# Attention rounds of a fused retention-and-MLP kernel: one state per round, whole rounds, and a ninth unit transposed by TensorE

## The chip, the core and the metric

The kernel runs on one core of a Trainium2 chip. A core has TensorE (PE in the profile; its weight loads are PEld), VectorE (DVE), ScalarE (ACT), GpSimd (POOL) and SyncE (SP), with 16 DMA engines. The time is the device time of one execution in microseconds (us). A comparison uses the median of several runs.

## What is computed

The reference is a retention layer without softmax, followed by an MLP with exact GELU. The shapes are q, k, v of (8, 8, 576, 64) (batch, heads, positions, head size), w_in (512, 2048), w_out (2048, 512) and an output of (4608, 512).

```python
scores = scale * np.matmul(q, k.transpose(0, 1, 3, 2))
gamma = 1.0 - 2.0 ** (-5.0 - np.arange(H))
rel = pos[:, None] - pos[None, :]
Dmat = np.where(rel >= 0, gamma[:, None, None] ** rel[None], 0.0)
attn_out = np.matmul(scores * Dmat[None], v)
x = attn_out.transpose(0, 2, 1, 3).reshape(B * S, H * D)
h = x @ w_in
out = (0.5 * h * (1.0 + erf(h / np.sqrt(2)))) @ w_out
```

## The kernel before

**Units and groups.** The 576 positions are cut into chunks of 128: four whole ones (ci = 0 to 3) and a tail of 64 (ci = 4). Batches go in pairs (bp = 0 to 3; j is the member of the pair). A unit is one chunk of one batch with all eight heads; the two tails of a pair share a unit. There are 36 units, numbered in the order of work, each 128 token columns of xT. Units 0, 1 are the chunk ci = 0 of bp = 0, and 2, 3 that of bp = 1. Then come 4 to 10 (rest of bp = 0), 11 to 17 (rest of bp = 1), 18 to 26 (bp = 2), 27 to 35 (bp = 3). Units with ci = 0 are called raw: they have no earlier chunk to add. Units 2 and 3 are also called kept, because their inputs stay loaded until bp = 1 begins. A group is the two units of one (bp, ci), or the tail alone.

**Steps of a unit.** Each has a function of its own:
- `load`: three DMAs issued by GpSimd bring q, k, v, cast to bf16.
- `turn` (TensorE into PSUM, line 294, then a copy by ScalarE or VectorE) or `turn_dma` (one DMA transpose issued by SP, line 303) makes qkT. The first N_PE_TR units take `turn`.
- `scores`: eight TensorE products (line 317) into two PSUM banks.
- `masked`: two VectorE products with the mask (line 332) give ret.
- `scaled_v`: VectorE scales v by a decay (line 342) and gives vh; the planner's time for it is called V. A raw unit's `inner` takes v itself, but the state needs its vh.
- `inner`: eight TensorE products of ret with the values (line 354) into a bank o_ps.
- `state`, once per group of two: 16 TensorE products (line 372) add k and vh to the running state in the bank u_ps, which is kept from ci = 0 to ci = 3. Two copies by ScalarE or VectorE (lines 284, 282) then bring it to u_sb.
- `cross`: four products with the state of the chunk before, or eight of half the width for a tail unit (line 406), added to o_ps.
- `evacuate`: o_ps goes to xT (line 426; for raw units by `either`, lines 282 and 284).

**The MLP.** The 4608 tokens form nine blocks of 512 columns, four units each. `mlp1` makes hT from w_in and xT (line 445), and ScalarE applies GELU (line 451). `mlp2` makes four output tiles per block from g and w_out (line 484), which ScalarE copies to o_sb (line 489) and SP sends out (line 492).

**The order.** Nothing is scheduled at run time. A planner in the kernel's Python code keeps a clock for each engine (T) and due times for loads, transposes, masks, copies and PSUM banks, and writes out the one order in which all engines get their instructions. At each step of its main loop it issues the first candidate that is due, else the next MLP piece whose inputs are due. The candidates before the change are X (cross and evacuate), U (a state), B (inner products, then all states that are due), A (scores of a group, with the inner products, states and crosses of the units before it) and T (a TensorE transpose). nT, nA, nB and nX count the units transposed, scored, with inner products and with crosses; units nB to nA - 1 are therefore scored and waiting for their inner products. A round is such a set issued together between two MLP pieces. "Early" means fewer than four units scored. "Stuck" means that the next MLP piece is due over 0.5 us from now. From block 2 on, A is offered only before the second or third piece of an `mlp2` output tile.

Two details matter below. Before the change, A issues every state whose V is planned at all:

```python
while u_due and state_at(*u_due[0]) < 1e8:
    state(*u_due[0])
```

And a stuck A takes one unit of the group:

```python
if early or stuck:
    g = g[:1]
```

There are eight PSUM banks, nine buffers for loaded units, eight for qkT and four for output tiles. Each state or tail unit that is done calls for the loads of later units (`reload`).

Of the kernel before, what the change touches and what calls it, by code (L numbers as in the profile page):

```python
# [17 lines left out]
def kernel(  # L18
# [16 lines left out]
    B, H, S, D = q.shape  # L35
# [9 lines left out]
    N_BLK = n_tok // TOK  # L45
# [13 lines left out]
    N_U = len(units)  # L59
# [5 lines left out]
    n = v_order.index(pair_of[1, 1][0])  # L65
    v_order[n:n] = kept

    N_PE_TR = 8
    N_LD = 9
    N_QKT = 8  # L70
    N_VH = 6
# [176 lines left out]
    def frees(n):  # L248
        got = sorted((x for x in banks if x not in held), key=lambda x: free_at[x])
        return got[:n]  # L250

    def free_time(n):
        got = frees(n)
        return free_at[got[-1]] if len(got) == n else 1e9
# [45 lines left out]
    def turn_dma(i):  # L300
        s = st[i]
        s["qkT"] = tr_pool.tile([128, 2, HP, 128], BF16, tag="qkT", name="qkT")
        nc.sync.dma_start(s["qkT"].rearrange("p j hp s -> p (j hp) s"),
                          loaded[i][0].rearrange("p j h d -> p (j h d)"), transpose=True)
        at = on("sp", 1.3, max(land["q", i], land["k", i]))
        turned[0] = max(turned[0], at) + 3.1
        sw[0] = max(sw[0], at) + 2.2
        s["T", 0] = s["T", 1] = turned[0] + 3.4

# [36 lines left out]
    def inner(i):  # L346
        bp, ci, j = units[i]
        s = st[i]
        s["o"] = bank([128, HP, 128], FP32, "o_ps")
        o = s["o"][1]  # L350
        vals = loaded[i][1] if i in raw else s["vh"]
        for hp in range(HP):
            for e in range(2):
                nc.tensor.matmul(o[64 * e:64 * e + 64, hp, :], lhsT=vals[:, 2 * hp + e, :], rhs=s["ret"][e][:, hp, :],  # L354
                                 start=(hp == 0), stop=(ci == 0 and hp == HP - 1), skip_group_check=True)
        s["B"] = pe(0.23, "col")
        s["Bdone"] = True
        if j is None:
            s_done.add(i)
        elif j == 1 and ci < NCI - 1 and (bp, ci) != (1, 0):  # L360
            u_due.append((bp, ci))
# [25 lines left out]
                reload()  # L387

    def state_at(bp, ci):
        return max(st[i].get("V", 1e9) if "Bdone" in st[i] else 1e9 for i in pair_of[bp, ci])  # L390

    def reload():
        ORDER.extend(f"{what}{next_load[0]}" for what in "qkv")
# [146 lines left out]
    def fire():  # L540
        nonlocal nT, nV
        now = T["pe"]
        while ORDER and T["pool"] <= now + 1.5:
            next_order()
        for key in [x for x in cast_due if land[x] <= now + 0.2]:
            dst, src = cast_due.pop(key)
            land[key] = either(0.44, land[key], dst, src) + SEM
        while later:
            n = next((n for n, x in enumerate(later) if x[0] <= now and T[x[1]] <= now + 0.05
                      and (x[1] == "dve" or later[0][3] is not make_args)), None)  # L550
            if n is None:
                break
            _, engine, dur, fn = later.pop(n)
            fn()
            on(engine, dur, now)
        while nV < N_U and nV < len(s_done) + N_VH and ("v", v_order[nV]) in land:
            i = v_order[nV]
            if land["v", i] + 0.1 > now or nA <= i or i in kept and nA < 8 or i in raw and T["dve"] > now:
                break
            scaled_v(i)  # L560
            nV += 1
        while (N_PE_TR <= nT < N_U and nT < nX + N_QKT - 1 and ("k", nT) in land
               and land["k", nT] + 0.3 <= now):
            turn_dma(nT)
            nT += 1
# [14 lines left out]
    while True:  # L580
        fire()
        now = T["pe"]
        acts = []

        def cand(ready, fn, *a):
            acts.append((ready, fn, a))

        pick = mlp_pick(1 if runs and runs[0] and runs[0][0][1] > 1 else 4)
        head = pick[1][0] if pick else None
        early = nA < 4  # L590
        stuck = bool(pick) and pick[0] > now + 0.5

        if nX < nB:
            bp, ci, j = units[nX]
            cand(u_ready.get((bp, ci - 1), 1e9) if ci else 0.0, "X")
        for key in u_due[:1]:
            if nA < 8 or nA == N_U or nB == nA:
                cand(state_at(*key), "U", *key)
        if nB < nA:
            g = [nB] if early else list(range(nB, nA))  # L600
            ready = max(max(st[i]["R"], land["v", i] if i in raw else st[i].get("V", 1e9)) for i in g)
            ready = max(ready, free_time(len(g) + (units[nB][1] == 0 and units[nB][2] == 0)))
            hurry = early or nA == N_U or stuck
            if not hurry and runs and runs[0]:
                kind, t = runs[0][0][0], runs[0][0][1]
                hurry = nB < 4 * t + 4 if kind == "1" else len(runs[0]) <= 6 and nB < 4 * t + 8
            if hurry:
                cand(ready, "B", g)
        if nA < N_U:
            g = [i for i in groups[group_of[nA]] if i >= nA]  # L610
            if early or stuck:
                g = g[:1]
            if all(("T", 1) in st[i] and ("T", 0) in st[i] for i in g):
                ready = max(max(st[i]["T", 0], st[i]["T", 1]) for i in g)
                back = [i for i in range(nB, nA) if st[i]["R"] <= now and (i in raw or "V" in st[i])]
                n = 2 * len(g) + len(back)
                ok = nA - nB <= 2
                if early or stuck:
                    cand(max(ready, free_time(2)) if ok else 1e9, "A", g, [])
                elif head is None or head[1] == 0 or head[0] == "2" and 4 <= head[3] <= 8 and head[1] < N_BLK - 1:  # L620
                    if len(back) == nA - nB and (head is None or nA + len(g) <= 4 * head[1] + AHEAD + 2 * (head[1] > 1)):
                        cand(max(ready, free_time(min(n, 8 - len(held))) - 0.3), "A", g, back)
        if nT < N_PE_TR and nT <= nA + 3:
            key = ("qk"[half], nT)
            if key in land and key not in cast_due:
                cand(max(land[key] + 0.05, free_time(1)), "T", nT, half)
        due = [a for a in acts if a[0] <= now]
        if due:
            _, kind, a = due[0]
            if kind == "X":  # L630
                cross(nX)
                evacuate(nX)
                nX += 1
            elif kind == "U":
                state(*a)
            elif kind == "B":
                for i in a[0]:
                    inner(i)
                    nB += 1
                while u_due and state_at(*u_due[0]) <= T["pe"]:  # L640
                    state(*u_due[0])
            elif kind == "A":
                g, back = a
                for i in back:
                    inner(i)
                    nB += 1
                while u_due and state_at(*u_due[0]) < 1e8:
                    state(*u_due[0])
                for i in g:
                    scores(i)  # L650
                    nA += 1
                for n, i in enumerate(g):
                    masked(i)
                    if n == 0:
                        for x in back:
                            cross(x)
                            evacuate(x)
                            nX += 1
            elif kind == "T":
                turn(*a)  # L660
                half = 1 - half
                nT += 1 - half
            continue
        if pick and pick[0] <= now:
            one = pick[1].pop(0)
            (mlp1 if one[0] == "1" else mlp2)(*one[1:])
            continue
        waits = [a[0] for a in acts] + ([pick[0]] if pick else [])
        soon = [x for x in (land[key] for key in cast_due)]
        if nV < N_U and ("v", v_order[nV]) in land and nV < len(s_done) + N_VH:  # L670
            soon.append(land["v", v_order[nV]] + 0.1)
        if N_PE_TR <= nT < N_U and ("k", nT) in land and nT < nX + N_QKT - 1:
            soon.append(land["k", nT] + 0.3)
        waits = [w for w in waits + soon if w > now and w < 1e8]
        if not waits:
            break
        gap = min(waits) - now
        if now < 16 and gap > 0.2:
            warm(max(1, round(gap / (0.43 if now < HOT else 0.23))))
        T["pe"] = max(T["pe"], min(waits))  # L680
# [31 lines left out]
```

## Time and profile before

| | before |
|---|---|
| median of 3 runs | 307.11 us (306.79 to 308.41) |
| the profiled execution | 307.32 us |
| its span, first to last instruction | 305.6 us |
| granted TensorE clock | 1.000 |
| TensorE busy | 296.2 us, 97% |
| ScalarE busy | 135.7 us, 44% |
| GpSimd busy | 113.8 us, 37% |
| VectorE busy | 99.7 us, 33% |
| largest groups: hT products, oT products | 127.9 and 123.5 us |

Busy time is the time in which at least one instruction of the engine was in flight. Matmuls overlap in the pipeline, so a product's own duration (0.38 us for 512 columns) is longer than the step from one to the next. What a block of work costs TensorE is therefore read from starts: the start of the next block less its own. In a line of waits, the two names are the waiting instruction and what ended the wait, and the numbers are the total, the count and the longest. Times in the timeline run from the span's start.

### The profile page before, as it was taken

The page shows a single profiled execution, that of the slowest core. Times are in us where ns is not written, and L with a number is a line of the kernel's source. Part 1 is how long each engine was busy: PE and PEld are TensorE (multiplying, and loading weights), DVE is VectorE, ACT ScalarE, POOL GpSimd, SP SyncE. Part 2 cuts the span into 40 slices and gives each one's busy share as a digit, 9 for nine tenths or more (in the row PEclk, how much of TensorE's full clock was granted, in tenths as well). Part 3 has the DMA queues.
Part 4 walks back from the last instruction along what each step waited for, and adds up shares of the span by engine and source line. Part 5 has one row for each costly group of instructions (what it writes and reads, how often), then busy time and mean ns, then how long its engine had stood idle before and what let it go on. Part 6 is the DMA issues. An engine that isn't in the chain of part 4 may idle for free. (4 is left out here: it accounts for less than half of the span.)

```text
span 305.6 us, 5759 instructions
## 1 busy us (share of the span) xinstructions
PE 296.2 (97%) x2391; PEld 160.3 (52%) x2425; DVE 99.7 (33%) x187; ACT 135.7 (44%) x243; POOL 113.8 (37%) x143
## 2 busy tenths in 40 slices
PE   7999999999999999999998999999989999999996
PEld 2589675765544554454444554444444544544445
DVE  6864325036530560055004670180008600400000
ACT  5575444433367234631562236422661266217611
POOL 8987895865349654200307944300000000000000
PEclk9999999999999999999999999999999999999999
DMA  9999999999999999995918999992000210010022
GB/s 140 164 182 188 176 183 151 216 169 175 172 176 145 154 186 158 176 116 115 126 21 55 159 150 174 172 157 94 9 2 34 66 39 2 34 71 34 0 65 75
DMA packets 154042, 35.77 MB, mean 117 GB/s; under 512 B 143008, under 2 KB 149536, under 8 KB 154016
## 3 DMA queue, kind: packets, MB, share of 16 engines
q0 software_dynamic: 116832, 18.10, 86.8%
q1 hardware_dynamic: 36144, 17.05, 28.9%
q8 instruction: 19, 0.31, 0.4%
q10 hardware_dynamic: 1040, 0.26, 0.4%
q14 instruction: 7, 0.06, 0.1%
HBM read 36.70 MB, written 9.44 MB: 151 GB/s over the span
## 5 line engine op out<-in xcount | busy, mean ns | idle before, releaser
L445 PE MATMUL hT<-xT,w_in 128*128 128x512 bf16 (+2 forms) x758 | 127.9, 325 | 0.8 <-DVE xT L426 0.2
L484 PE MATMUL oT<-w_out,g 128*128 128x512 bf16 x538 | 123.5, 379 | 1.2 <-issue 0.2
L451 ACT ACTIVATE g<-hT 128x512 bf16<-128x512 f32 (+1 forms) x152 | 86.9, 574 | 48.1 <-PE hT L445 47.6
L445 PEld LDWEIGHTS <-w_in 128*128 128x128 bf16 x768 | 69.6, 98 | 56.8 <-DVE xT L426 0.4
L484 PEld LDWEIGHTS <-g 128*128 128x128 bf16 x560 | 53.4, 98 | 60.2
L489 ACT COPY o_sb<-oT 128x512 f32<-128x512 f32 x35 | 20.4, 586 | 92.8 <-PE oT L484 74.8
L332 DVE TENSOR_TENSOR ret<-sc,msk 128x512 bf16<-128x512 f32 x56 | 35.5, 684 | 63.0 <-PE sc L317 63.0
L219 POOL DMA_DIRECT2D qk_ld<-in_q_dram x31 | 27.9, 901 | 42.2 <-DMA qkT<-qk_ld 15.8
L219 POOL DMA_DIRECT2D v_ld<-in_v_dram x32 | 28.8, 900 | 13.0 <-DMA qk_ld<-in_q_dram 8.4
L219 POOL DMA_DIRECT2D qk_ld<-in_k_dram x31 | 28.0, 903 | 5.6 <-DMA v_ld<-in_v_dram 3.7
L342 DVE TENSOR_TENSOR vh<-v_ld,dv 128x512 bf16<-128x512 bf16 x36 | 23.4, 684 | 1.9 <-DMA v_ld<-in_v_dram 1.9
L284 ACT CAST u_sb<-u_ps 64x512 bf16<-64x512 f32 x26 | 15.1, 579 | 15.5 <-PE u_ps L372 15.2
L332 DVE TENSOR_TENSOR ret<-sc,near 128x512 bf16<-128x512 f32 x16 | 10.3, 685 | 35.4 <-PE sc L317 35.4
L426 DVE TENSOR_TENSOR xT<-o_ps,dqT 128x512 bf16<-128x512 f32 x28 | 18.2, 683 | 10.8 <-PE o_ps L406 10.8
L282 DVE CAST u_sb<-u_ps 64x512 bf16<-64x512 f32 x6 | 4.1, 688 | 45.7 <-PE u_ps L372 45.6
L317 PE MATMUL sc<-qkT 64*128 64x128 bf16 x288 | 12.3, 220 | 0.0
L354 PEld LDWEIGHTS <-vh 128*64 128x64 bf16 x224 | 6.8, 109 | 7.4 <-issue 5.9
L317 PEld LDWEIGHTS <-qkT 64*128 64x128 bf16 x288 | 8.2, 95 | 3.2 <-issue 1.1
L354 PE MATMUL o_ps<-ret,vh 128*64 128x128 bf16 x224 | 9.7, 223 | 0.0
L372 PE MATMUL u_ps<-vh,qk_ld 128*64 128x64 bf16 x256 | 6.8, 196 | 2.8 <-ACT u_sb L284 2.5
L406 PE MATMUL o_ps<-qkT,u_sb 128*128 128x128 bf16 (+1 forms) x128 | 9.3, 214 | 0.0
L215 POOL DMA_DIRECT2D v_ld<-in_v_dram x8 | 5.4, 678 | 10.0 <-DMA v_ld<-in_v_dram 3.9
(51 smaller groups left out, 99.8 us busy)
## 6 DMA issues: line engine op xcount, KB each, us to landing
out_dram<-o_sb SPq DMA_DIRECT2D x31, 256.0 KB, 4.1
v_ld<-in_v_dram POOLq DMA_DIRECT2D x32, 128.0 KB, 8.8
qk_ld<-in_k_dram POOLq DMA_DIRECT2D x31, 128.0 KB, 9.1
qk_ld<-in_q_dram POOLq DMA_DIRECT2D x31, 128.0 KB, 8.7
w_in<-in_moe_w_in_dram POOLq DMA_DIRECT2D x8, 256.0 KB, 7.5
w_out<-in_moe_w_out_dram POOLq DMA_DIRECT2D x8, 256.0 KB, 8.2
out_dram<-o_sb SPq DMA_DIRECT2D x9, 128.0 KB, 2.4
qk_ld<-in_q_dram POOLq DMA_DIRECT2D x8, 64.0 KB, 11.6
```

The lines of the kernel that those rows point to most:

```text
L219: nc.gpsimd.dma_start(dst, src[2 * bp + j, :, ci * C:ci * C + C, :].rearrange("h s d -> s h d"))
L284: nc.scalar.copy(dst, src)
L317: nc.tensor.matmul(got[e][1][:, hp, :], lhsT=qkT[sl, 1, hp, :], rhs=qkT[sl, 0, hp, :], start=True, stop=True)
L332: nc.vector.tensor_tensor(r, t, by, op=ALU.mult)
L342: nc.vector.tensor_tensor(vh, loaded[i][1], dv[:, :, ci:ci + 1].to_broadcast([128, H, D]), op=ALU.mult)
L354: nc.tensor.matmul(o[64 * e:64 * e + 64, hp, :], lhsT=vals[:, 2 * hp + e, :], rhs=s["ret"][e][:, hp, :], start=(hp == 0), stop=(ci == 0 an ...
L406: nc.tensor.matmul(o[:, hp, cols], lhsT=u[:, jj, hp, :], rhs=s["qkT"][:, 0, hp, cols], start=False, stop=(hp == HP - 1), skip_group_check= ...
L426: nc.vector.tensor_tensor(dst, o, by, op=ALU.mult)
L445: nc.tensor.matmul(hT[:, m, :], lhsT=w[:, cc, o:o + 128], rhs=xT[:, cc, t * TOK + lo:t * TOK + hi], start=(cc == 0), stop=(cc == N_DM - 1))
L451: nc.scalar.activation(g_tiles[t, m0 // 2][:, m0 % 2:m0 % 2 + n, lo:hi], hT, AF.Gelu)
L484: nc.tensor.matmul(oT, lhsT=g_tiles[t, m // 2][:, m % 2, cols], rhs=w_out_sb[m // 2][:, m % 2, :], start=(m == 0), stop=(m == N_DF - 1))
L489: nc.scalar.copy(o_sb, oT)
```

## The change

1. N_PE_TR goes from 8 to 9: unit 8 is transposed by TensorE, no longer by a DMA.
2. The planner's due time for a DMA transpose is later when many loads are queued in front of it.
3. A state counts as due only when the state before it has been copied to u_sb (`state_at`), and a round issues at most one state.
4. `scaled_v` of a raw unit may be put on VectorE when that engine is planned up to 2 us behind (once nA > 8); before, VectorE had to be idle.
5. Candidates A and B become one, S. It issues the inner products of all waiting units, one state, the scores of the next group, the mask of the group's first unit, the crosses of the waiting units and the other mask. When stuck, the masks all come after the crosses.
6. A round wants R (mask) and V due for all waiting units, raw ones too. A stuck step after the start takes the whole group. Rounds are also offered in the second cut of block 1's `mlp1`.

```diff
-    N_PE_TR = 8
+    N_PE_TR = 9
...
-        turned[0] = max(turned[0], at) + 3.1
+        busy = sw[0] > at + 1.0
+        turned[0] = max(max(turned[0], at) + 3.1, turned[0] + 4.4 * busy, at + 5.4 * busy)
...
     def state_at(bp, ci):
-        return max(st[i].get("V", 1e9) if "Bdone" in st[i] else 1e9 for i in pair_of[bp, ci])
+        at = u_ready.get((bp, ci - 1), 1e9) if ci else 0.0
+        return max([at] + [st[i].get("V", 1e9) if "Bdone" in st[i] else 1e9 for i in pair_of[bp, ci]])
...
-            if land["v", i] + 0.1 > now or nA <= i or i in kept and nA < 8 or i in raw and T["dve"] > now:
+            if land["v", i] + 0.1 > now or nA <= i or i in kept and nA < 8 or i in raw and T["dve"] > now + 2.0 * (nA > 8):
...
+        g, scored = [], 1e9
+        if nA < N_U:
+            g = [i for i in groups[group_of[nA]] if i >= nA]
+            if early or stuck and nA < 8:
+                g = g[:1]
+            if all(("T", 1) in st[i] and ("T", 0) in st[i] for i in g):
+                scored = max(max(st[i]["T", 0], st[i]["T", 1]) for i in g)
+        back = list(range(nB, nA))
         if nB < nA:
...
+            ready = max(max(st[i]["R"], land["v", i] if i in raw and nA < 8 else st[i].get("V", 1e9)) for i in back)
+            ready = max(ready, free_time(len(back) + first_o))
...
             if hurry:
-                cand(ready, "B", g)
...
+                n = len(back) + first_o + 2 * len(g)
+                along = not early and nA >= 4 and scored <= now and len(frees(n)) == n and free_time(n) <= now + 0.3
+                cand(ready, "S", g if along else [], back)
+        if g and scored < 1e8:
             if early or stuck:
...
+                cand(max(scored, free_time(2 * len(g))) if nA - nB <= 2 else 1e9, "S", g, [])
+            elif head is None or head[1] == 0 or head[1] == 1 and head[0] == "1" and head[4] > 0 or head[0] == "2" and 4 <= head[3] <= 8 and head[1] < N_BLK - 1:
+                if (all(st[i]["R"] <= now and st[i].get("V", 1e9) <= now + 0.3 for i in back)
+                        and (head is None or nA + len(g) <= 4 * head[1] + AHEAD + 2 * (head[1] > 1))):
+                    n = 2 * len(g) + len(back)
+                    cand(max(scored, free_time(min(n, 8 - len(held))) - 0.3), "S", g, back)
...
+            elif kind == "S":
                 g, back = a
                 for i in back:
                     inner(i)
                     nB += 1
-                while u_due and state_at(*u_due[0]) < 1e8:
+                if back and u_due and state_at(*u_due[0]) <= T["pe"] + 0.3 * (nA >= 8):
                     state(*u_due[0])
                 for i in g:
                     scores(i)
                     nA += 1
...
+                if not stuck:
+                    for i in g[:1]:
+                        masked(i)
+                if not early and nX == nB - len(back):
+                    for x in back:
+                        cross(x)
+                        evacuate(x)
+                        nX += 1
+                for i in g[not stuck:]:
+                    masked(i)
```

More of the change, by code (lines that the diff above doesn't have):

```diff
@@ L598 @@
                 cand(state_at(*key), "U", *key)
-        if nB < nA:
-            g = [nB] if early else list(range(nB, nA))
-            ready = max(max(st[i]["R"], land["v", i] if i in raw else st[i].get("V", 1e9)) for i in g)
-            ready = max(ready, free_time(len(g) + (units[nB][1] == 0 and units[nB][2] == 0)))
+        g, scored = [], 1e9
[6 more added lines that the diff above has]
+        back = list(range(nB, nA))
+        if nB < nA:
+            if early:
+                back = [nB]
+            first_o = units[nB][1] == 0 and units[nB][2] == 0
+            ready = max(max(st[i]["R"], land["v", i] if i in raw and nA < 8 else st[i].get("V", 1e9)) for i in back)
+            ready = max(ready, free_time(len(back) + first_o))
             hurry = early or nA == N_U or stuck
@@ L607 @@
             if hurry:
-                cand(ready, "B", g)
-        if nA < N_U:
-            g = [i for i in groups[group_of[nA]] if i >= nA]
+                n = len(back) + first_o + 2 * len(g)
+                along = not early and nA >= 4 and scored <= now and len(frees(n)) == n and free_time(n) <= now + 0.3
+                cand(ready, "S", g if along else [], back)
+        if g and scored < 1e8:
             if early or stuck:
[L612 to L622, printed above, removed]
+                cand(max(scored, free_time(2 * len(g))) if nA - nB <= 2 else 1e9, "S", g, [])
[4 more added lines that the diff above has]
+                    cand(max(scored, free_time(min(n, 8 - len(held))) - 0.3), "S", g, back)
         if nT < N_PE_TR and nT <= nA + 3:
@@ L635 @@
                 state(*a)
[L636 to L642, printed above, removed]
+            elif kind == "S":
                 g, back = a
@@ L651 @@
                     nA += 1
-                for n, i in enumerate(g):
-                    masked(i)
[L654 to L658, printed above, removed]
+                if not stuck:
[7 more added lines that the diff above has]
+                for i in g[not stuck:]:
+                    masked(i)
             elif kind == "T":
```

## Prediction, made before the change was run

> **What bounds the kernel now.** I read the page first.
>
> ```profile
> PE 296.2 (97%) x2391; PEld 160.3 (52%) x2425; DVE 99.7 (33%) x187; ACT 135.7 (44%) x243; POOL 113.8 (37%) x143
> ...
> PEclk9999999999999999999999999999999999999999
> ```
>
> TensorE is occupied for 97% of the span at full granted clock, every other engine under half. So the time is the sum of what TensorE issues, plus the places where it stands still; anything on another engine counts only if TensorE ends up waiting for it. Next, TensorE's waits, which say where it stands still.
>
> ```profile
> PE u_ps L372 <- ACT u_sb L284: 2.5, 2, 1.3
> PE warm L577 <- DVE zeros L100: 1.2, 1, 1.2
> PE u_ps L372 <- PE o_ps L354: 0.3, 1, 0.3
> PE hT L445 <- DVE xT L426: 0.2, 1, 0.2
> ```
>
> After the start there is one wait of size, twice: a state update (u_ps) waiting for ScalarE's copy of the state before. No line is a wait for a load or a transposed input: DMA, 90% busy or more in most slices of the first two thirds, is hidden. Third, TensorE's timeline gives the attention blocks between MLP products. A block's cost is the start of the next MLP product less the start of its own first product (columns: start, duration, engine, line, operation).
>
> ```profile
> 40.52 0.61 PE L294 MATMUL qk_ps<-ident,qk_ld 128*128 128x128 bf16 x8
> 40.96 1.04 PE L445 MATMUL hT<-xT,w_in 128*128 128x256 bf16 x8
> ...
> 136.08 0.64 PE L354 MATMUL o_ps<-ret,v_ld 128*64 128x128 bf16 x16
> 136.65 0.62 PE L317 MATMUL sc<-qkT 64*128 64x128 bf16 x16
> 137.20 9.67 PE L484 MATMUL oT<-w_out,g 128*128 128x512 bf16 x43
> ...
> 161.48 0.64 PE L354 MATMUL o_ps<-ret,vh 128*64 128x128 bf16 x16
> 161.95 0.42 PE L372 MATMUL u_ps<-vh,qk_ld 128*64 128x64 bf16 x16
> 163.64 0.44 PE L372 MATMUL u_ps<-vh,qk_ld 128*64 128x64 bf16 x16 [1.27 <-ACT u_sb L284]
> 164.02 0.62 PE L317 MATMUL sc<-qkT 64*128 64x128 bf16 x16
> 164.57 0.62 PE L406 MATMUL o_ps<-qkT,u_sb 128*128 128x128 bf16 x8
> 165.24 6.86 PE L484 MATMUL oT<-w_out,g 128*128 128x512 bf16 x31
> ...
> 172.03 0.64 PE L354 MATMUL o_ps<-ret,vh 128*64 128x128 bf16 x16
> 172.50 0.42 PE L372 MATMUL u_ps<-vh,qk_ld 128*64 128x64 bf16 x16
> 172.85 0.62 PE L317 MATMUL sc<-qkT 64*128 64x128 bf16 x16
> 173.40 0.62 PE L406 MATMUL o_ps<-qkT,u_sb 128*128 128x128 bf16 x8
> 174.07 1.24 PE L484 MATMUL oT<-w_out,g 128*128 128x512 bf16 x5
> ```
>
> A normal whole round (two inner products, one state, two scores, two crosses) takes 174.07 - 172.03 = 2.04 us. The round at 161.48 takes 3.76: two states stand in it, and the second writes the bank that ScalarE still copies. The round of the ci = 0 pair before it (136.08) takes 1.12 and has no state. The same pair of rounds comes back at 201.06 (1.12) and 226.46 (3.76).
>
> **The state rounds: -2.9 us.** The ci = 0 pairs at issue are 18, 19 (bp = 2) and 27, 28 (bp = 3). Three edits act together. scaled_v of such a pair no longer waits for VectorE to be idle, a round waits for V of its pair, and a round issues one state, if the state before it is already copied. So state (2,0) moves from the round at 161.48 into the one at 136.08, and by the next round its two copies (0.58 us each) have been done for long. A state within a round costs 0.25 (172.50 to the scores, 0.35, less the 0.11 that changing tile mode costs: eight scores take 0.33, sixteen 0.55, so 0.22 a unit and 0.11 fixed). Before: 1.12 + 3.76 = 4.88; after: 1.37 + 2.04 = 3.41. That saves 1.47 each, 2.9 for both. What is late next: the moved state reads vh of its pair. If VectorE is behind, the state waits, and the scores, crosses and all MLP products queued behind it wait too. The planner allows 0.3 us of lateness; the nearest rows are four weight-load waits on vh, 1.5 us in all, none over 0.4. I bound it by 0 and 0.4 per round and take 0.1 each, **+0.2**.
>
> What else moves with the state: its reloads. GpSimd waited 15.1 us at 147 to 162 for that state before it issued the next loads; they now go about 25 us earlier, into slices in which DMA was not full (tenths 5, 9 and 1 from 138 to 160). Nothing waits for these loads, so this is slack and no time; SP's transposes of them come earlier among the output DMAs, which four o_sb buffers, one used per 3.45 us of products, cover. If that cover went, an output copy would wait behind one transpose issue (1.2 to 4.2 us on SP). The state bank is held some 25 us longer, through an MLP stretch of 64 products: such a stretch took 13.82 us with a state bank held (84.59 to 98.41) and 13.81 without (116.62 to 130.43), so zero.
>
> **Whole rounds between 65 and 135 us: -0.8 us.** Blocks before, from the timeline: 0.55 (8, 9 scored), 1.82, 1.72 (10, then 11, 12), 2.00 (11, 12, then 13 alone, with 0.23 idle for xT), 0.91 (13; 14), 1.38 (14; 15, 16), 2.03 (15, 16; 17, slow by 0.21 against its twin of 1.82), 1.36. Sum 11.77. After, following the planner's branches by hand: 8, 9 are scored in the second cut of block 1's MLP1 (0.55), then 1.82, then 10 with 11, 12 as one round (1.38, as at 103.83), then 11, 12 (1.28, as at 51.26), 13, 14 scored together (0.55), one whole round (2.04), 1.82, 1.36. Sum 10.80, so -0.97. Between 11, 12 and MLP1 of block 2 lies the copy to xT: if no MLP2 piece is left to hide it, about 0.6 more are idle, unless 13 and 14 are scored in it. Bounds -0.4 and -1.0; I take -0.8, near the end that the rows add up to.
>
> **Scores of 8 and 9 some 4 us earlier: 0.** Their transposes must have landed. Unit 9's landed at 60.6 and its scores stood at 65.7; the new slot is near 61.8. One transpose fewer lies ahead of it in DMA. Transposes took 3.0 to 11.3 us to land, 8.2 this one, so the bounds are 0 and 1.5 us of standing still, with all MLP1 behind it; I take 0, since the slot stays behind the row's landing time.
>
> **Ninth unit by TensorE: +0.45 us.** Eight transposes took 40.96 - 40.52 = 0.44, without a change of mode; two copies (0.42 on VectorE or 0.59 on ScalarE) fall where VectorE is 29% and ScalarE 45% busy (40 to 60 us) and 4 us before the scores are due. They take two of eight PSUM banks for a microsecond: bounds 0.44 and 0.9 should an MLP1 product wait for a bank. Removed: one DMA transpose (issue 1.33 on SP, 41.74 to landing 50.15). The loads queued behind it should come about 2 us earlier. TensorE waits for none of them: nothing gained.
>
> [...]
>
> The constants turned and busy only delay the planner's idea of a transpose; units from 14 on were scored over 9 us after landing, so zero.
>
> **Sum.** -2.9 + 0.2 - 0.8 + 0 + 0.45 = -3.05. The profiled execution took 307.32 us (span 305.6 and 1.7 around it): 304.3. The median of the runs is 0.2 lower; I predict 304.0 for a median. About 0.5%, 1.5 us, is what a measurement of this kernel can tell from no change.
>
> **Rivals.**
> *Late transposes.* The earlier scores of 8, 9, or 13, 14 wait in TensorE's queue for the DMA: 1 to 2 us. For: transposes landed up to 11.3 us after issue, and unit 14's landed at 84.4, beside where 13, 14 could now be scored. Against: one transpose less ahead. 305 to 306. Chance 0.11.
> *The state does not move.* VectorE, with masks, xT and vh of one round queued (139.48 is where vh ran before), stays too late for the ci = 0 round, and the two waits only change their place: 307.3 - 0.8 + 0.45 = 307.0, median 306.8. Chance 0.08.
> *State lag, slower.* One state per round also means that a missed one stays a round behind. Then each cross waits for the two copies just started: 1.18 + 0.2 less 0.55 of scores, about 0.85 a round, in up to four rounds of each of two sequences: 6.8, in place of 2.9. It decides from four such rounds on; with all eight, 307.3 + 6.8 - 2.9 - 0.8 + 0.45 = 310.9. For: the while loop that caught up is gone. Against: rounds lie 5 us and more apart, and copies take 1.2. Chance 0.07.
> Main case: 0.74, 303.2 to 305.0.
>
> **How the numbers follow.** Low end: no vh wait (-0.2), all of -0.97, and a little of idle issue, 303.0. High end: through the late transposes, 306.2; left out are the last two rivals (0.15) and some 0.05 below. Under 305.6 lie the main case and about half of the late transposes: faster 0.80. Same: the other half and most of the second rival, 0.12. Slower 0.08.
>
> **What would show it.** Right: the u_ps wait on u_sb gone; 16 state products between inner products and scores in both ci = 0 rounds, block near 1.37; the next round near 2.04; no eight-score block of unit 13; 72 transposes on line 294's counterpart instead of 64. Wrong: a wait of sc on a DMA transpose, of o_ps on u_sb in every round, or of u_ps on vh over 0.4; or MLP blocks that lengthen.

## The result

| | before | changed |
|---|---|---|
| median | 307.17 us (306.79 to 308.41) | 303.75 us (303.28 to 304.56) |
| runs | 4 | 4 |
| profiled execution | 307.32 us | 303.70 us |
| its span | 305.6 us | 301.9 us |

The ratio of the times is 0.9885, with a 95% interval of 0.9849 to 0.992. The prediction was 304.0 us, between 303.0 and 306.2. On another chip the changed kernel came out at 304.22 us beside 307.37 for the one before, a ratio of 0.9894 (0.988 to 0.9909).

The first two lines are from the page of the changed kernel.

```profile
PE 295.3 (98%) x2400; PEld 160.6 (53%) x2433; DVE 99.1 (33%) x188; ACT 136.6 (45%) x244; POOL 114.1 (38%) x143
...
PEclk9999999999999999999999999999999999999999
```

TensorE is still the bound (98% busy) and still at full granted clock (1.000). It was busy 0.9 us less in a span 3.7 us shorter. Most of the gain is therefore standing still that is gone, as TensorE's waits say (total, count, longest):

```profile
PE warm L579 <- DVE zeros L100: 1.2, 1, 1.2
PE oT L486 <- issue: 0.3, 2, 0.2
PE u_ps L373 <- PE o_ps L355: 0.3, 1, 0.3
```

The two waits of u_ps for the copy to u_sb, 2.5 us together, have no successor in this list. TensorE's timeline shows the rounds (start, duration, engine, line, operation):

```profile
40.30 0.61 PE L294 MATMUL qk_ps<-ident,qk_ld 128*128 128x128 bf16 x8
...
42.48 0.39 PE L294 MATMUL qk_ps<-ident,qk_ld 128*128 128x128 bf16 x4
42.70 1.04 PE L447 MATMUL hT<-xT,w_in 128*128 128x256 bf16 x8
43.58 0.39 PE L294 MATMUL qk_ps<-ident,qk_ld 128*128 128x128 bf16 x4
43.80 1.04 PE L447 MATMUL hT<-xT,w_in 128*128 128x256 bf16 x8
...
98.76 0.62 PE L318 MATMUL sc<-qkT 64*128 64x128 bf16 x16
99.31 4.49 PE L486 MATMUL oT<-w_out,g 128*128 128x512 bf16 x19
...
130.66 0.41 PE L355 MATMUL o_ps<-ret,vh 128*64 128x128 bf16 x8
...
136.22 0.64 PE L355 MATMUL o_ps<-ret,v_ld 128*64 128x128 bf16 x16
136.69 0.42 PE L373 MATMUL u_ps<-vh,qk_ld 128*64 128x64 bf16 x16
137.04 0.62 PE L318 MATMUL sc<-qkT 64*128 64x128 bf16 x16
137.81 8.58 PE L486 MATMUL oT<-w_out,g 128*128 128x512 bf16 x39 [0.16 <-issue]
...
161.00 0.64 PE L355 MATMUL o_ps<-ret,vh 128*64 128x128 bf16 x16
161.47 0.42 PE L373 MATMUL u_ps<-vh,qk_ld 128*64 128x64 bf16 x16
161.82 0.62 PE L318 MATMUL sc<-qkT 64*128 64x128 bf16 x16
162.38 0.62 PE L408 MATMUL o_ps<-qkT,u_sb 128*128 128x128 bf16 x8
163.05 6.85 PE L486 MATMUL oT<-w_out,g 128*128 128x512 bf16 x31
...
226.56 6.85 PE L486 MATMUL oT<-w_out,g 128*128 128x512 bf16 x31
```

Unit 8's transposes are the two groups of four at 42.48 and 43.58, each 0.22 us from its start to the next product's. Units 13 and 14 are scored together at 98.76. The round of the ci = 0 pair at 136.22 now holds a state, and the round at 161.00 holds one instead of two: 163.05 - 161.00 = 2.05 us, where 3.76 stood.

One thing has to be known for reading blocks. The trace lacks some matmul records: the page of the changed kernel has 560 weight loads of line 486 but 537 products, and a later profile of the same kernel has 560 of both. Where the first MLP product after a block is missing, the block reads one product, 0.21 us, too long. That is so at 137.81 (39 records of 40 products) and at 163.05 (31 of 32), and at 165.24 and 174.07 in the trace of before (31 of 32 and 19 of 20). In the profile of the run with the state rule alone, where the record is there, a whole round is 1.84 us (161.78 to 163.62), not 2.04. Differences between blocks that miss the same record hold.

The shortening of 3.7 us, cut at points that are the same in both traces (the points of the kernel before that were not shown yet):

```profile
131.39 0.41 PE L354 MATMUL o_ps<-ret,vh 128*64 128x128 bf16 x8
...
230.22 6.86 PE L484 MATMUL oT<-w_out,g 128*128 128x512 bf16 x31
```

| stretch | before | changed | difference |
|---|---|---|---|
| start to the transposes of unit 7 | 40.52 | 40.30 | -0.22 |
| from there to the round of unit 17 (131.39, 130.66) | 90.87 | 90.36 | -0.51 |
| to the MLP product after the round of 20, 21 (165.24, 163.05) | 33.85 | 32.39 | -1.46 |
| to the one after the round of 29, 30 (230.22, 226.56) | 64.98 | 63.51 | -1.47 |
| to the end | 75.38 | 75.34 | -0.04 |

The -0.51 contains the 0.44 of the ninth unit; without it, whole rounds gave -0.95. The -0.22 belongs to no edit. TensorE's instructions up to there come in the same order. The first MLP product began at 14.48 before and at 14.26 in the changed kernel, and between 13.9 and 15.1 us in the profiles of the other runs.

### The profile page after: what moved, and what is told of

Same layout as the page of the kernel before. It is cut to its first block, busy times and chain, and to the rows that moved or that the text cites. A ratio compares the mean times of both kernels' runs of the same rounds, so it can differ in the third digit from the quotient of the medians.

```text
span 301.9 us, 5775 instructions
## 1 busy us (share of the span) xinstructions
PE 295.3 (98%) x2400; PEld 160.6 (53%) x2433; DVE 99.1 (33%) x188; ACT 136.6 (45%) x244; POOL 114.1 (38%) x143
## 4 chain that ended last, share of the span: by engine, by line
PE 98%; issue 1%; DVE 0%; ACT 0%
PE hT L447 41%; PE oT L486 40%; PE o_ps L355 4%; PE sc L318 3%; PE o_ps L408 3%; PE qk_ps L294 2%; PE warm L579 2%; PE warm L572 1%; PE u_ps L373 1%; PE oT L473 1%; DVE zeros L100 0%; ACT o_sb L477 0%
## 5 line engine op out<-in xcount | busy, mean ns | idle before, releaser
L219 POOL DMA_DIRECT2D v_ld<-in_v_dram x32 | 28.6, 893 | 14.1 <-DMA qk_ld<-in_q_dram 4.1
L219 POOL DMA_DIRECT2D qk_ld<-in_k_dram x31 | 27.9, 902 | 7.8 <-DMA v_ld<-in_v_dram 6.0
L284 ACT CAST u_sb<-u_ps 64x512 bf16<-64x512 f32 x29 | 16.8, 580 | 21.1 <-PE u_ps L373 19.8
L282 DVE COPY qkT<-qk_ps 128x512 bf16<-128x512 bf16 x14 | 5.8, 422 | 8.5 <-PE qk_ps L294 8.4
L215 POOL DMA_DIRECT2D qk_ld<-in_k_dram x8 | 5.5, 693 | 6.7 <-DMA qk_ld<-in_k_dram 3.7
L408 PEld LDWEIGHTS <-u_sb 128*128 128x128 bf16 x128 | 6.5, 98 | 1.5
```

The source lines that it names most:

```text
L219: nc.gpsimd.dma_start(dst, src[2 * bp + j, :, ci * C:ci * C + C, :].rearrange("h s d -> s h d"))
L284: nc.scalar.copy(dst, src)
L408: nc.tensor.matmul(o[:, hp, cols], lhsT=u[:, jj, hp, :], rhs=s["qkT"][:, 0, hp, cols], start=False, stop=(hp == HP - 1), skip_group_check= ...
```

## The experiments

### The state rule, alone and undone

The kernel before got the slack for VectorE and the wait for V, the latter limited to the pairs of bp = 2 and 3:

```diff
-  ... or i in raw and T["dve"] > now:
+  ... or i in raw and T["dve"] > now + 2.0 * (nA > 8):
...
-  back = [i for i in range(nB, nA) if st[i]["R"] <= now and (i in raw or "V" in st[i])]
+  back = [i for i in range(nB, nA) if st[i]["R"] <= now and ("V" in st[i] if nA < 18 or i not in raw
+          else st[i].get("V", 1e9) <= now + 0.3)]
```

Expected:

> The kernel before, with the state rule alone: the vh of a ci = 0 pair may be put on VectorE when that engine is planned 2 us behind, and from unit 18 on a round wants V of such a pair, so that state (2,0) and (3,0) stand in the rounds of their own pairs. Order, transposes and the other rounds stay as before. Theory (the double-state rounds were worth 1.47 us each): 307.2 - 2.9 = 304.3 us, blocks of 1.37 and 2.04 us in place of 1.12 and 3.76, no wait of u_ps on u_sb. Rival (the gain of the change came from its whole rounds, and the wait of 1.3 us only moves to another place): 306.5 to 307.2 us.

Measured: 304.56 us beside 307.48 (ratio 0.9909, 0.9894 to 0.9925), -2.92 us. Its timeline, with all records there, has the pair of rounds at 1.37 (here) and 1.84:

```profile
137.00 0.64 PE L354 MATMUL o_ps<-ret,v_ld 128*64 128x128 bf16 x16
137.47 0.42 PE L372 MATMUL u_ps<-vh,qk_ld 128*64 128x64 bf16 x16
137.82 0.62 PE L317 MATMUL sc<-qkT 64*128 64x128 bf16 x16
138.37 0.39 PE L484 MATMUL oT<-w_out,g 128*128 128x512 bf16 x1
```

The other way round, the changed kernel lost the rule from unit 18 on:

```diff
-  ... or i in raw and T["dve"] > now + 2.0 * (nA > 8):
+  ... or i in raw and T["dve"] > now + 2.0 * (8 < nA < 18):
...
-  if (all(st[i]["R"] <= now and st[i].get("V", 1e9) <= now + 0.3 for i in back)
+  if (all(st[i]["R"] <= now and (nA >= 18 and i in raw or st[i].get("V", 1e9) <= now + 0.3) for i in back)
...
-  if back and u_due and state_at(*u_due[0]) <= T["pe"] + 0.3 * (nA >= 8):
+  more = bool(back)
+  while more and u_due and state_at(*u_due[0]) <= (T["pe"] + 0.3 * (nA >= 8) if nA < 18 else 1e8):
       state(*u_due[0])
+      more = nA >= 18
```

> The changed kernel with the state rule undone from unit 18 on: ci = 0 pairs don't wait for V, and a round issues all states whose V is planned. Everything else as changed. Theory: two rounds of 3.76 us with two states each come back, 303.75 + 2.9 = 306.7 us. Rival: whole rounds alone carry the gain, 303.8 us.

Measured: 306.99 us beside 307.48 (0.9985, 0.9974 to 0.9995). That is 3.2 us above a variant with the changed kernel's blocks on the same chip (303.82, below). The wait is back, two times 1.3 us: "PE u_ps L373 <- ACT u_sb L284: 2.6, 2, 1.3". The state rule is shown from both sides, at 2.9 to 3.2 us.

### One state per round, a round late: the slower rival

```diff
-  if back and u_due and state_at(*u_due[0]) <= ...
+  if back and not (nA >= 18 and back[0] in raw) and u_due and state_at(*u_due[0]) <= ...
```

> The changed kernel, but the rounds of the ci = 0 pairs of bp = 2 and 3 issue no state, and the rule of one state per round stays: every later state of the two sequences comes one round late, just ahead of the cross that reads its copy. This is the prediction's slower rival, made on purpose. Its price there: each of 7 rounds waits for two copies of 0.58 us in series plus about 0.2, less the scores between (0.55 for two units, 0.33 for one): about 0.85 or 1.07 a round, 5 x 0.85 + 2 x 1.07 = 6.4, so 303.75 + 6.4 = 310.1 us, with o_ps waiting for u_sb in each such round. The other theory (the copies are hidden behind the scores and the pipeline): under 305 us.

Measured: 310.57 us (1.0105, 1.0089 to 1.0122), 6.75 us above 303.82. TensorE's waits and the first such round:

```profile
PE o_ps L408 <- ACT u_sb L284: 5.8, 7, 1.0
```

```profile
160.70 0.64 PE L355 MATMUL o_ps<-ret,vh 128*64 128x128 bf16 x16
161.17 0.42 PE L373 MATMUL u_ps<-vh,qk_ld 128*64 128x64 bf16 x16
161.52 0.62 PE L318 MATMUL sc<-qkT 64*128 64x128 bf16 x16
162.87 0.62 PE L408 MATMUL o_ps<-qkT,u_sb 128*128 128x128 bf16 x8 [0.73 <-ACT u_sb L284]
163.33 0.38 PE L486 MATMUL oT<-w_out,g 128*128 128x512 bf16 x1
```

The round takes 163.33 - 160.70 = 2.63 instead of 1.84, so 0.79 more, with 0.85 expected. The mechanism of the slower rival is real and its price was right. The changed kernel does not meet its condition, because there the round waits for V.

### Which of the three edits of the state rule is needed

```diff
-  ... or i in raw and T["dve"] > now + 2.0 * (nA > 8):
+  ... or i in raw and T["dve"] > now + 0.0 * (nA > 8):
```

> The changed kernel with one constant: scaled_v of a ci = 0 unit again waits until VectorE is planned idle (2.0 becomes 0.0). The prediction said that three edits act together. Theory A (all three are needed): the state falls out of the ci = 0 rounds or these rounds are delayed enough to cost, 305 us or more. Theory B (it is enough that a round waits for V; it only comes one MLP piece later): 303.75 us within 0.3%, same blocks.

Measured: 303.82 us (0.9882, 0.9866 to 0.9898), with the same blocks as the changed kernel. Theory B holds: letting VectorE be 2 us behind is not needed. The run with the state rule alone had no rule of one state per round and gained its 2.9 us all the same. The wait of a round for V is in both runs. That wait without the other two edits was not run. The prediction's "three edits act together" was too much by one at least.

### The ninth unit

Its price was enlarged: `turn` of unit 8 issued its transposes nine times.

```diff
+        if i == 8:
+            for _ in range(8):
+                for hp in range(HP):
+                    nc.tensor.transpose(t[:, hp, :], qk[:, jj, 2 * hp:2 * hp + 2, :], ident1)
```

> The changed kernel with the TensorE transposes of unit 8 issued nine times into the same bank, 64 more; nothing else moves. The price of the ninth unit by itself, enlarged. Theory A (TensorE pays each in full and pipelined, 0.44 us for eight): 8 x 0.44 = 3.5 us more, 307.3 us. Rival 1 (part of it falls into waits that TensorE has anyway): under 306.5 us. [...]

Measured: 307.51 us, 3.3 above the changed kernel beside it:

> The changed kernel itself, on the chip of the runs beside it, so that they are compared like with like: a ratio to the kernel before of 0.988, about 303.8 us.

That kernel took 304.22 us (0.9894). In the timeline, 36 transposes take 44.12 - 42.11 = 2.01 us:

```profile
42.11 0.39 PE L294 MATMUL qk_ps<-ident,qk_ld 128*128 128x128 bf16 x4
42.34 1.95 PE L299 MATMUL qk_ps<-ident,qk_ld 128*128 128x128 bf16 x32
44.12 1.04 PE L451 MATMUL hT<-xT,w_in 128*128 128x256 bf16 x8
```

So 0.056 us each. All of it is paid: from the transposes of unit 7 to the last output products this trace has 39.93 and 298.61, the one beside it 40.79 and 295.90, so 3.57 us more, which is 64 times 0.056. A tenth unit shows whether there is more to win:

```diff
-    N_PE_TR = 9
+    N_PE_TR = 10
```

> The changed kernel with N_PE_TR = 10: unit 9 too is transposed by TensorE. Theory A (the ninth unit is worth its price for its transposed inputs, and a tenth brings more of it): 303.3 us or less. Theory B (with nine, TensorE waits for no transpose any more, so a tenth only costs its 0.44 us): 304.2 us, no waits either way.

Measured: 304.56 us (0.9901, 0.9885 to 0.9917), 0.34 above the 304.22 beside it, with intervals that overlap. Theory A's gain is not there, and TensorE waits for nothing after its start: Theory B. And with the ninth back on DMA:

```diff
-    N_PE_TR = 9
+    N_PE_TR = 8
```

> The changed kernel with N_PE_TR = 8: unit 8 goes back to a DMA transpose. Theory A (prices add up): 0.44 us less, 303.4 us. Theory B (the ninth unit is paid on TensorE to bring the transposed inputs forward in the planner's order): 11, 12 are scored in a round of their own and one MLP2 output later, so their copies to xT come late and block 2 waits 1.5 to 2.5 us for them: 305.2 to 306 us, with hT waiting for xT near 84 us.

Measured: 304.67 us (0.9919, 0.9894 to 0.9945). Neither theory's number, but B's mechanism at a smaller size. From the transposes of unit 7 to the scores of 13, 14, this kernel takes 100.57 - 41.03 = 59.54 us and the changed one 98.76 - 40.30 = 58.46: 1.08 longer, although 0.44 of transposes are gone. The reason stands ahead of block 2:

```profile
83.42 0.41 PE L355 MATMUL o_ps<-ret,vh 128*64 128x128 bf16 x8 [0.25 <-DVE vh L343]
84.02 0.41 PE L355 MATMUL o_ps<-ret,vh 128*64 128x128 bf16 x8 [0.19 <-DVE vh L343]
84.27 0.42 PE L373 MATMUL u_ps<-vh,qk_ld 128*64 128x64 bf16 x16
84.62 0.62 PE L408 MATMUL o_ps<-qkT,u_sb 128*128 128x128 bf16 x8
85.80 1.02 PE L447 MATMUL hT<-xT,w_in 128*128 128x512 bf16 x4 [0.56 <-DVE xT L428]
```

Units 11 and 12 were scored at 79.85 instead of 75.8, their vh and xT came late, and the block takes 2.38 us, after a wait of 0.25, where the changed kernel's takes 1.28 without a wait (read 1.50 in its trace, with the missing record). In this trace, then, the ninth unit is paid in TensorE time and returned in the order. In the ratios to the kernel before it is worth 0.8 to 1.0 us, and the intervals overlap (0.9894 to 0.9945 here, 0.9849 to 0.992 there), so its size is not settled.

The same edit alone on the kernel before (8 to 9) does harm:

> The kernel before with N_PE_TR = 9 and nothing else. Theory A (each edit has a price of its own; the terms add up): eight transposes more on TensorE, 0.44 us, 307.4 + 0.4 = 307.8 us. Theory B (the edit also moves the planner's order, and the old rules deal badly with it): the state (1,0) comes in one round with (1,1), units 13, 14 and 15 are scored one by one ahead of block 2, and their masks stand on VectorE before the copies to xT that the MLP waits for; some 4 us more, 311 to 312 us, with hT waiting for xT near 85 us.

Measured: 316.08 us (1.0284, 1.0261 to 1.0308). Theory B has the direction, but the size (311 to 312) and half of the mechanism were wrong. TensorE's waits hold most of the loss:

```profile
PE u_ps L372 <- ACT u_sb L284: 3.8, 3, 1.3
PE sc L317 <- DMA qkT<-qk_ld: 3.8, 1, 3.8
```

A third double state stands ahead of block 2. Then the scores of unit 15 were put in TensorE's queue at 86.5, with its DMA transpose landing at 90.35, and all of MLP1 waited behind them. By the code, two things can make that order: the old rule for stuck steps, which takes single units, and the old due time, which puts a transpose earlier than it lands. No run separates them. In the long wait the granted clock fell to 0.50 as well (see the last section).

### Early scores and the due time of DMA transposes

The prediction booked both at zero. First, no rounds in the second cut of block 1's MLP1:

```diff
-  elif head is None or head[1] == 0 or head[1] == 1 and head[0] == "1" and head[4] > 0 or head[0] == "2" and ...
+  elif head is None or head[1] == 0 or head[0] == "2" and ...
```

> The changed kernel without rounds in the second cut of block 1's MLP1: 8, 9 are scored at the start of block 1's MLP2 again, as before. Theory A (the prediction: scoring them earlier is worth nothing by itself): 303.75 us. Theory B (the later rounds move with it; the state (1,0) misses the round of unit 10 and stands just before (1,1), which waits for its copy): one wait of about 1 us, 304.6 to 305.2 us.

Measured: 306.33 us (0.9969, 0.9955 to 0.9983), so 2 us or more above the changed kernel, more than either theory. State (1,0) missed the round of unit 10, the cross of 11, 12 waited 1.3 us for its copy, and the MLP waited 0.6 for xT:

```profile
PE o_ps L408 <- ACT u_sb L284: 1.3, 1, 1.3
...
PE hT L447 <- DVE xT L428: 0.6, 1, 0.6
```

The two waits, 1.28 and 0.56 us in its timeline, account for 1.8 us. That is the state lag of the prediction's slower rival, met once. The profiled execution is the slowest of ten, at 307.39 us: its granted clock fell for a while as well (0.994 over the whole execution, see the last section), which that of the others, 305.88 to 306.78 us at 1.000, did not. Next, the old due time:

```diff
-  busy = sw[0] > at + 1.0
-  turned[0] = max(max(turned[0], at) + 3.1, turned[0] + 4.4 * busy, at + 5.4 * busy)
+  turned[0] = max(turned[0], at) + 3.1
```

> The changed kernel with the old due time of DMA transposes (3.1 us apart whatever is queued). The planner then scores 8, 9 near 59 us, 10 near 65 and 11, 12 near 73 us, while in the changed kernel's trace units 9, 10 and 12 landed at 59.2, 65.3 and 75.3. Theory A (the prediction booked the due times at nothing): 303.75 us. Theory B (TensorE's queue waits for the DMA, the prediction's late transposes): 0.3 to 0.5 us at 10 and up to 2 us at 11, 12, all MLP products behind it: 305 to 306 us, with waits of sc on the transposes of qkT.

Measured: 306.29 us over ten executions, 306.09 without one of 310.12 whose granted clock was 0.994 (0.9954, 0.9933 to 0.9974, without that one), about 2 us more. TensorE's queue does wait for the DMA:

```profile
58.61 0.40 PE L317 MATMUL sc<-qkT 64*128 64x128 bf16 x8
60.05 0.40 PE L317 MATMUL sc<-qkT 64*128 64x128 bf16 x8 [1.04 <-DMA qkT<-qk_ld]
...
75.79 0.40 PE L317 MATMUL sc<-qkT 64*128 64x128 bf16 x8 [1.23 <-DMA qkT<-qk_ld]
```

The first wait is at 9, not at 10 as expected; the sum is the same. Both edits back, the fourth corner of a square of N_PE_TR and due time:

> The changed kernel with both N_PE_TR = 8 and the old due time of DMA transposes, which with the runs of each alone makes a square of two by two. Theory A (prices add): the 0.4 us of TensorE saved and the waits for late transposes of the old due time, about 2.4 us: 305.8 us. Theory B (with the unit on DMA the planner's slots move too; 8, 9 would be scored near 59.4 us with unit 9 landing near 60.6, and 13, 14 ahead of block 2 near 84 us with unit 14 landing near 84.5): two waits of sc on transposes, 1.2 and 0.5 to 1 us, against 0.9 saved: 304.2 to 305.2 us.

Measured: 304.66 us (0.9904, 0.9887 to 0.9922), as Theory B said, with waits of sc on transposes of 0.97 and 0.22 us at 9 and 14. The square reads, as ratios to the kernel before: 0.9885 to 0.9894 (nine, new due time), 0.9919 (eight, new), 0.9954 (nine, old), 0.9904 (eight, old). The ninth unit needs the longer due time: with the old one it costs 1.5 us beside the corner with neither, clear of the intervals. That the pair together is worth its place is not shown: it is 0.3 to 0.6 us ahead of the corner with neither, and these intervals overlap. No variant beat the changed kernel beyond its interval.

## Why the prediction was right, step by step

- **State rounds, -2.9.** Measured -1.46 and -1.47 in the changed kernel's trace, -2.92 us alone, 3.2 undone. The step, its place and its price held.
- **Late vh, +0.2.** Measured nothing: no weight load or product waits for vh in the changed kernel. The bound of zero was the right end.
- **Whole rounds, -0.8.** Measured -0.95, near the -0.97 that the rows added up to. Some of the blocks that were added up hold the missing record, 0.21 us too much each. It was four of them in the sum before and four in the sum after, which is luck; so the difference holds. The order worked out by hand is the one in the trace, and one MLP2 piece was left after 11, 12 to hide the copy to xT, so the 0.2 held back for that was not needed.
- **Ninth unit, +0.45.** The TensorE time was right (0.44). "Nothing gained" was not: relative to the order that the new rules make, the unit on DMA costs 1.08 us net in the trace and 0.8 to 1.0 in the ratios. The sum was unharmed, because the order worked out by hand already had the unit on TensorE.
- **Early scores, 0.** No wait, as said. But the slot is what lets state (1,0) into its round; without it 2 us are lost.
- **Due times, 0.** Wrong as a statement. Without the longer due time, two waits of 1.0 and 1.2 us come. The late-transposes rival was the right mechanism (its places were 9 and, unnamed, 12, not 13 and 14), and this edit is what kept it away: units 9 and 12 landed at 59.15 and 75.25, their scores stood at 61.56 and 75.77. The prediction had looked at the landing of 9 and of 14, not of 12. That the 0.5 us left there was enough is luck as far as its reasoning goes.
- **The sum.** Left over are -0.15 (whole rounds), -0.2 (vh) and -0.22 from the start, which no edit explains and which lies within the scatter of the start: -3.05 forecast, -3.62 in the profiled executions, -3.42 in the medians.

## What to carry to other kernels

When one engine is full, cut its timeline into blocks between the big products and compare like with like: the odd block (3.76 beside 2.04) names the wait, and its price is the difference. Work out the new order before adding up terms, and then don't price the edits one by one: a due time or a slot that looks free may be what keeps a wait away (here 1.04 and 1.23 us with the old due time, 1.28 and 0.56 us without the slot), and the same edit alone on the old kernel cost 8.8 us. An accumulator that is copied out between updates wants its update one round before the reader, and a planner that lets it slip by one round pays at every later round (here seven waits, 5.8 us in all, in the run with one state per round, a round late).

## What the runs showed of the hardware

The granted clock halved in two profiled executions: within one wait of 3.79 us, and after two of 1.28 and 0.56 us. These rows are from the kernel before with the ninth unit alone, in stretches of 2 us (stretch, length, busy time and instructions of PE, PEld, DVE, ACT, POOL, then the granted clock, DMA share and GB/s):

```profile
86.00:88.00 2.00, 0.60 (x10) 0.43 (x8) 1.96 (x4) 0.00 (x0) 1.42 (x2) 1.00 1.98 180
88.00:90.00 2.00, 0.00 (x0) 0.00 (x0) 2.00 (x4) 0.00 (x0) 1.21 (x2) 0.58 1.11 100
90.00:92.00 2.00, 1.24 (x10) 0.70 (x11) 2.00 (x5) 0.00 (x0) 0.87 (x1) 0.50 1.57 264
92.00:94.00 2.00, 2.00 (x6) 0.71 (x5) 1.70 (x3) 0.60 (x1) 1.75 (x2) 0.50 2.07 156
94.00:96.00 2.00, 2.00 (x8) 0.71 (x7) 0.00 (x0) 0.60 (x2) 1.41 (x3) 0.72 3.51 142
96.00:98.00 2.00, 2.00 (x11) 0.92 (x10) 0.00 (x0) 1.47 (x3) 1.84 (x3) 1.00 2.74 148
```

TensorE's last product before the long wait ends at 86.6. The means of the slices (0.58, 0.50, 0.50, 0.72) put half the clock from about 88.3 to 95.1, if it stood at 1.00 or 0.50 and at nothing between. So it falls 1.7 us into the wait and comes back 6.8 us later, though TensorE is full again from 92 on; six products of hT fit (92 to 94) where eleven do at full clock (96 to 98). The profiled execution of the kernel with late scores shows the same around waits of only 1.28 and 0.56 us within 3 us:

```profile
84.00:86.00 2.00, 0.96 (x10) 0.70 (x11) 1.09 (x2) 0.42 (x1) 0.79 (x1) 1.00 2.09 158
86.00:88.00 2.00, 2.00 (x22) 0.85 (x20) 0.54 (x2) 0.60 (x1) 1.84 (x3) 0.56 2.52 142
88.00:90.00 2.00, 2.00 (x7) 0.72 (x6) 0.34 (x1) 1.18 (x2) 0.04 (x1) 0.58 0.87 219
90.00:92.00 2.00, 2.00 (x11) 0.88 (x9) 0.00 (x0) 1.19 (x2) 1.53 (x2) 1.00 1.57 196
```

Here the clock, read the same way from 0.56 and 0.58, is half from about 86.2 to 89.7, for 3.4 us. Not every execution of this kernel has it: over the whole execution the granted clock was 0.994 in this one and 1.000 in the nine others, which have the same order of instructions. With the ninth unit alone it was 0.988 or 0.989 in all four executions.

In their profiles, a single wait of 1.28 us (the double states), seven of up to 1.0 us spread over 100 us (the state lag) and two of 1.0 and 1.2 us 15 us apart (the old due time) left the clock at 1.0; one of the ten executions with the old due time had 0.994. What sets the two lengths, 6.8 and 3.4 us, why these waits cost clock and those did not, and why one execution of ten lost its clock and the others did not, no run shows.
